# Second attention's last eight turns: rows of the output projection in portions of six products, the next row split during the portions, begun sooner

## The chip, the cores and the metric

The kernel runs on one core of one Trainium2 chip. The metric is the device time of one execution in microseconds (us); three runs were timed. A profiled execution gives a trace of every engine: PE (TensorE, with its weight loads as PEld), DVE (VectorE), ACT (ScalarE), POOL (GpSimd), and SP, which here only issues DMAs.

## The reference

Four layers with residuals on one sequence of 2048 tokens and 640 channels: attention, state space convolution, attention, convolution. The attention is the layer that matters here:

```
def _A_ref(x, wqkv, wo):
    B, S, D = x.shape
    H = 32
    Dh = D // H
    qkv = (lambda x, *d: x.transpose(*d))((x @ wqkv).reshape(B, S, 3, H, Dh), 2, 0, 3, 1, 4)
    q, k, v = qkv[0], qkv[1], qkv[2]
    scores = jnp.einsum("bhqd,bhkd->bhqk", q, k) * (Dh ** -0.5)
    p = _softmax(scores, axis=-1)
    o = jnp.einsum("bhqk,bhkd->bhqd", p, v)
    return (lambda x, *d: x.transpose(*d))(o, 0, 2, 1, 3).reshape(B, S, D) @ wo
...
x = x + _A_ref(_layernorm(x, axis=-1), A_wqkv, A_wo)
x = x + _B_ref(_layernorm(x, axis=-1), B_log_A_real, B_A_imag, B_C_real, B_C_imag, B_log_dt, B_D_skip)
x = x + _A_ref(_layernorm(x, axis=-1), A_wqkv, A_wo)
x = x + _B_ref(_layernorm(x, axis=-1), B_log_A_real, B_A_imag, B_C_real, B_C_imag, B_log_dt, B_D_skip)
```

32 heads of 20 channels; `_B_ref` is a long convolution, done by transforms. The last product, `o @ wo`, is the output projection that the change moves about.

## The kernel before

**Turns.** The attention works on groups of four heads (`g`, 0 to 7) and quarters of the queries (`qb`, 0 to 3, 512 queries each). A group and a quarter are a *turn*; there are 32, and the last eight of the second attention go through the quarters with groups 6 and 7 alternating, so that whole quarters of the sequence become final one after the other. A turn has 16 steps over the keys, of 128 keys each. A step makes two score tiles `S` (two heads each, 128 keys by 1024, eight small matmuls), ACT takes the exponential of each into a tile `pt`, and a value group `pa<-pt,V` sums the four heads' outputs. `S` has two buffers in PSUM, so a third score waits until the first exponential has read its tile. `pt` has seven buffers. A turn therefore has 32 scores, 32 exponentials and 16 value groups.

**Order.** PE's instructions are chained in the order in which they are written, and the writer goes by a plan: the class `Plan` keeps estimated times `plan.pe`, `plan.act`, `plan.dve`, which are advanced by fixed costs (0.22 for a score, 0.92 for an exponential, 0.865 for a value group). After each score, `fill` writes a value group that is due and then, with `slot(plan.act - 0.5)`, pieces of other work as long as the planned PE time, with the piece's cost, stays 0.5 under the planned ACT time. What such a piece is comes from a generator in `todo`: first the projections of the attention itself (`jobs`), and in the last turns of the second attention the rows of the output projection (`rows_out`). Work of DVE, POOL and SP that has a due time is kept in the list `later`, which `drain_later` empties.

**Rows of the output projection.** A *row* `s` (0 to 15) is 128 tokens. The attention's scaled outputs are stored to DRAM as `ot` (channels by tokens). `Rows.load` fetches a row's channels into a tile `otl`, in two parts: channel blocks 0 to 2 and 3 to 4 (of five blocks of 128), since the second part needs groups 6 and 7. `Rows.split` cuts it into two float parts `oh` and `ol` (a copy and a subtraction on DVE). With the weights cut likewise into `woh` and `wol` a block takes three products, `ol` by `woh`, `oh` by `woh`, `oh` by `wol`, for each half of 320 output columns: 18 products for a part of three blocks, 12 for one of two, 30 for a whole row. They add up in a PSUM tile `m`, and DVE adds each half to the residual `x`. When both parts of a row are done, `stats_of` and `normalise` make its layer norm on DVE for the convolution that follows (`uhx`, `ulx`).

`rows_out` begins 30 planned microseconds after it is set up, yields a portion of four products to `slot` at a time, and prices it so:

```
part_ = mm[k:k + 4]
cost = 0.25 + 0.147 * len(part_)
yield t0, cost, k > 0, tuple(hf for hf in range(2) if k <= half * hf < k + 4)
```

Before it comes `end_jobs`, where `prefetch` loads the weights `wo`; their five splits are put into `later` at 8, 12, 16, 20 and 24 planned microseconds.

**Behind the turns.** The last block of the attention (group 7, last quarter) is scaled by `at_once`: a matmul with `dsel` spreads the sums, DVE takes a reciprocal, scales `oc`, and POOL issues the stores to `ot`. Then `out_proj` makes what is left of the projection, in order of rows, into PSUM tiles `po`: a row's `ol` products first, then its `oh` products, the splits now by ACT (`oh`) and DVE (`ol`), two row parts loaded ahead, and each finished row is normalised with the help of ACT (`u`, `uhx`). The last four rows, 12 to 15, need the last block. `psx` is the first stage of the convolution, which takes the normalised rows two by two.

Of the kernel before, what the change touches and what calls it, by code (L numbers as in the profile page):

```python
# [29 lines left out]
NA, NB = 32, 64  # L30
LV = [1.0, 2.0, 4.0, 8.0, 16.0, 32.0, 64.0, 128.0, 256.0, 512.0, 1024.0, 1536.0]
PB = 7
AHEAD = ((0, 0.0), (110, 6.0), (236, 32.0), (364, 59.0), (600, 95.0), (724, 134.0))
BLOCKS = ((0, 128), (128, 32), (160, 128), (288, 128), (416, 128), (544, 96))
NBLK = len(BLOCKS)
# [52 lines left out]
def mha_s4d_kernel(ctx, tc, x_in, wqkv, wo, lar, aim, cr, ci, ldt, dsk,  # L88
# [23 lines left out]
    def pst(pool, *a, **k):  # L112
        return ps_[pool].tile(*a, **k)
# [318 lines left out]
    def attention(x, stats):  # L432
# [522 lines left out]
        def end_jobs():  # L955
# [18 lines left out]
                xpools.pop().__exit__(None, None, None)  # L974
            rest = []
            made = prefetch(x, rest)
            later.extend((plan.pe + (6.0 + 1.5 * n if first_layer else 8.0 + 4.0 * n), f) for n, f in enumerate(rest))
            later.sort(key=lambda e: e[0])
            return made

        def fill(j):

            if ready:
                t = max(ready[0][0] + 0.15, 0.0 if ready[0][3] else sums_[0])
                if t <= plan.pe + 0.1 or j and len(ready) > 2:
                    plan.on_pe(0.0, t)
                    values(*ready.pop(0)[1:])
            while slot(plan.act - 0.5):
                pass
            drain_later()  # L990
            weave()
# [59 lines left out]
        def rows_out(rows, x, woh, wol):  # L1051

            def ask():
# [1 line left out]
                if item:  # L1055
                    rows.load(item)
                return plan.pe + 6.0
            t, done, parts_done = plan.pe + 30.0, [], set()
            while rows.left or rows.loaded:
                yield t, 0.0, False, ()  # L1060
                if stop:
                    return
                if not rows.loaded:
                    t = ask() - (0.0 if rows.loaded else 4.0)
                    continue
                (s, c0, c1), oh, ol = rows.split(ve.tensor_copy)
                t0, t = plan.dve + 0.2, ask()
                mm = [(hf, a, m, ct) for hf in range(2) for ct in range(c0, c1) for a, m in ((ol, woh), (oh, woh), (oh, wol))]
                half, k, pos = len(mm) // 2, 0, [None, None]
                while k < len(mm):  # L1070
                    part_ = mm[k:k + 4]
                    cost = 0.25 + 0.147 * len(part_)
                    yield t0, cost, k > 0, tuple(hf for hf in range(2) if k <= half * hf < k + 4)
                    plan.on_pe(cost)
                    for hf, a, m, ct in part_:
                        if k % half == 0:
# [6 lines left out]
                    while done:  # L1083
                        hf = done.pop()
                        xs = x[:, s, 320 * hf:320 * hf + 320]
                        evac = lambda: ve.tensor_add(xs, xs, pos[hf])
                        emptied(*((None, evac) if hf else (evac,)))
                if s in parts_done:
                    stats_of(x, s, rows.mv[:, s, :])
                    rows.whole.add(s)  # L1090
                    normalise(rows, x, s)
                parts_done.add(s)

        last[0] = None
        tail, rows, stop = None, None, []
        every = {NBLK - 1, ("v", 3)}
        NG = H // 4
        turns = [(g, qb) for g in range(NG) for qb in range(4)]
# [2 lines left out]
        for n, (g, qb) in enumerate(turns):  # L1101
# [4 lines left out]
            if tail is not None and rows is None and (n == len(turns) - 1 or not first_layer):  # L1106
# [6 lines left out]
                    first = []  # L1113
                else:
                    todo[0], head[0] = rows_out(rows, tail[0], tail[2], tail[3]), None
            pa = [pst("A", [P, 512], F32, tag=f"pa{r}", name=f"pa{r}") for r in range(2)]
            g2, qb2 = turns[n + 1] if n + 1 < len(turns) else (g, 0)
            for kt in range(NI):
# [22 lines left out]
            values(*r_[1:])  # L1141
        if not first_layer:
            stop.append(True)
            first = []
            while head[0] is not None and head[0][1]:
                slot()
            for s in range(NI):
                two = [(s, 0, 3), (s, 3, NCT)]
                if set(two) <= set(rows.left):
# [644 lines left out]
```

## Time and profile before

| | us |
|---|---|
| runs | 2646.05, 2641.08, 2644.88 |
| median | 2644.88 |
| profiled execution: span from its first to its last instruction | 2647.0 |
| second attention's turns, from the first exponential's start | 1469.26 |
| its last eight turns, from the first exponential's start | 2203.02 |

The page of the profile states the span of the profiled execution and no other time of it.

```profile
PE 2492.4 (94%) x52388; PEld 1409.8 (53%) x52388; DVE 1519.5 (57%) x3430; ACT 2344.0 (89%) x2763; POOL 801.7 (30%) x1230
...
PE   6899999999999999899898999999999998999898
...
ACT  7899999999999999655665899999999999999574
```

The first line has each engine's busy time, share of the span and instructions. In the strips each digit is the busy share of one fortieth of the span (66 us), in tenths. The last eight turns are slices 34 to 37 of 40, counted from 1, and the projection behind them is slice 38. In rows of the trace, `x8` counts instructions, a time in us comes first, and brackets hold the idle time of the engine before the row and what ended it. The kernel computes in fp32 with two passes for some products, so that the profile counts 16 instructions of a value group where the program has 8.

### The profile page before, as it was taken

To read this page: it belongs to the slowest core of one execution; us is meant where nothing else is said; L and a number is where in the kernel's file an instruction comes from. 1 tells how busy PE (TensorE), PEld (TensorE's weight loads), DVE (VectorE), ACT (ScalarE), POOL (GpSimd) and SP (SyncE) were. 2 spreads that over 40 slices of the span, in tenths; PEclk is the share of its full clock that TensorE was granted. 3 is DMA by queue.
4 is the path that set the end of the run, shared out by engine and by line. 5 is a ranking of instruction groups with operands and counts; after the bars stand their busy time and mean duration, and the time that the engine had idled before them with its cause. 6 is when DMAs were issued, how large, how long until landed. Compare 5 with 4: busy or idle time off the path is not lost.

```text
span 2647.0 us, 118800 instructions
## 1 busy us (share of the span) xinstructions
PE 2492.4 (94%) x52388; PEld 1409.8 (53%) x52388; DVE 1519.5 (57%) x3430; ACT 2344.0 (89%) x2763; POOL 801.7 (30%) x1230
## 2 busy tenths in 40 slices
PE   6899999999999999899898999999999998999898
PEld 3444444454444444587896544454444443444898
DVE  7587777777765887577786323232232222143875
ACT  7899999999999999655665899999999999999574
POOL 1123333233323332111681122222222223222285
PEclk9999999999999999999999999999999999999999
DMA  6522222322222221654652111121121113222466
GB/s 206 189 53 77 68 74 62 82 65 63 61 54 59 53 63 38 234 206 163 213 173 64 47 53 50 51 60 45 45 66 39 50 34 87 71 66 61 137 190 184
DMA packets 188158, 241.99 MB, mean 91 GB/s; under 512 B 43504, under 2 KB 128816, under 8 KB 186224
## 3 DMA queue, kind: packets, MB, share of 16 engines
q1 hardware_dynamic: 151936, 188.28, 22.6%
q0 software_dynamic: 35696, 46.01, 7.4%
q8 instruction: 413, 6.77, 1.1%
q14 instruction: 113, 0.93, 0.1%
HBM read 158.16 MB, written 76.00 MB: 88 GB/s over the span
## 4 chain that ended last, share of the span: by engine, by line
ACT 59%; PE 20%; issue 10%; DVE 3%; DMA 2%; POOL 1%; SPq 0%; ACTq 0%; POOLq 0%; DVEq 0%
ACT pt L78 57%; PE psy L1430 3%; PE pa L903 2%; PE psv L1430 2%; PE po L193 2%; PE psx L1430 2%; PE S L868 2%; PE pst L1452 1%; PE pkx L193 1%; PE pv L586 1%; PE m L620 1%; PE pkt L196 1%; PE pq L773 1%; DMA kb<-khb 1%; DMA kop<-ks 1%
## 5 line engine op out<-in xcount | busy, mean ns | idle before, releaser
L78 ACT ACTIVATE pt<-S 128x1024 f32<-128x1024 f32 x2048 | 1927.7, 1033 | 27.9 <-PE S L868 15.5
L903 PE MATMUL pa<-pt,V 64*32 64x512 f32 x16384 | 1096.9, 589 | 1.4 <-DVE oc L78 1.4
L868 PE MATMUL S<-qop,kop 61*32 61x512 f16 x16384 | 877.2, 380 | 82.7 <-ACT pt L78 67.8
L868 PEld LDWEIGHTS <-kop 61*32 61x32 f16 x16384 | 366.9, 89 | 737.3 <-issue 619.2
L903 PEld LDWEIGHTS pa<-pt,V 64*32 64x32 f32 x16384 | 312.7, 106 | 72.0 <-issue 8.6
L78 POOL DMA_DIRECT2D dn<-oc x248 | 122.7, 501 | 574.2 <-DVE oc L78 574.1
L78 DVE TENSOR_SCALAR qc<-m 128x512 f32<-128x512 f32 (+1 forms) x68 | 46.8, 688 | 312.0 <-PE m L620 312.0
L78 POOL DMA_DIRECT2D db<-dn x248 | 125.4, 512 | 141.5 <-DMA dn<-dr 136.9
L78 POOL DMA_DIRECT2D ot<-oc x256 | 130.5, 517 | 88.4 <-DVE oc L78 55.5
L620 PE MATMUL m<-xl,wh 64*32 64x512 f16 x2560 | 143.8, 376 | 0.3 <-issue 0.3
L620 PE MATMUL m<-xh,wh 64*32 64x512 f16 x2560 | 144.1, 378 | 0.0
L620 PE MATMUL m<-xh,wl 64*32 64x512 f16 x2560 | 143.8, 377 | 0.0
L78 DVE COPY oc<-pa 128x512 f32<-128x512 f32 x64 | 44.2, 690 | 172.9 <-PE pa L903 168.9
L78 ACT COPY xt<-pst 128x1024 f16<-128x1024 f16 x80 | 81.3, 1016 | 60.8 <-PE pst L1452 60.8
L620 PEld LDWEIGHTS <-wh 64*32 64x32 f16 x5120 | 90.3, 93 | 73.3 <-issue 30.8
L78 POOL DMA_DIRECT2D dn<-dr x62 | 34.6, 558 | 287.3 <-DVE dr L78 248.6
L1480 POOL TENSOR_TENSOR kb<-t,kb 128x512 f32<-128x512 f32 x76 | 97.2, 1280 | 65.2 <-DVE t L78 40.8
L78 DVE TENSOR_SCALAR V<-m 128x160 f32<-128x160 f32 x64 | 20.7, 324 | 163.4 <-PE m L586 163.4
L78 DVE TENSOR_TENSOR kb<-ktab 128x512 f32<-128x512 f32 x160 | 106.2, 683 | 0.0
L586 PEld LDWEIGHTS <-xh 128*128 128x128 f16 x960 | 79.7, 98 | 46.7 <-issue 31.4
L1480 POOL TENSOR_TENSOR ka<-ka,kb 128x512 f32<-128x512 f32 x76 | 97.5, 1283 | 6.0
L337 PEld LDWEIGHTS m<-kb,ka 128*32 128x32 f32 x3840 | 60.8, 109 | 71.0 <-issue 52.4
(312 smaller groups left out, 3936.4 us busy)
## 6 DMA issues: line engine op xcount, KB each, us to landing
ka<-kha SPq DMA_DIRECT2D x80, 256.0 KB
kb<-khb SPq DMA_DIRECT2D x80, 256.0 KB
db<-dn POOLq DMA_DIRECT2D x248, 64.0 KB, 3.2
kop<-ks SPq DMA_DIRECT2D x176, 80.0 KB
kpw<-wd POOLq DMA_DIRECT2D x60, 192.0 KB, 3.9
qop<-qs SPq DMA_DIRECT2D x256, 40.0 KB
ot<-oc POOLq DMA_DIRECT2D x256, 40.0 KB, 3.0
kha<-kn SPq DMA_DIRECT2D x20, 512.0 KB
```

The lines of the kernel that those rows point to most:

```text
L78: made = f(out, *a, **k)
L193: chain(te.matmul(*a, **k))
L196: chain(te.transpose(*a, **k))
L337: chain(te.matmul(ps[32 * j:32 * j + 32, c8, :], a[n][:, ch, :], b[n][:, dd, :], start=(n == 0), stop=(n == 2), tile_position=(0, 32 * j)))
L586: chain(te.matmul(ps[:, :n], a_[:, ct, sl], m[:, ct, :], start=(k == 0), stop=(k == 14)))
L620: chain(te.matmul(ps[r][32 * t:32 * t + 32, :], a_[rows, ct, 32 * u:32 * u + 32], m[rows, ct, 512 * v:512 * v + 512], start=(k == 0), stop ...
L773: te.matmul(pq, a_[:, ct, :], m[:, ct, sl], start=(n == 0), stop=(n == 14))
L868: chain(te.matmul(S[32 * t:32 * t + 32, 512 * r:512 * r + 512], kt_[rows, kc + 32 * t:kc + 32 * t + 32], qt[rows, :], start=True, stop=Tru ...
L903: chain(te.matmul(pa[r][32 * j:32 * j + 32, :], V[rows, kt, VP * h:VP * h + 32], pts[j // 2][rows, 512 * (j % 2):512 * (j % 2) + 512], sta ...
L1430: at("pe", te.matmul(*a, **k))
L1452: at("pe", te.transpose(pt[:, k, g, :], of_group(x1[k], 4 * q + g), id16))
L1480: at("pool", getattr(ge, f)(*a))
```

## The change

Portions of the projection in the turns are six products instead of four (`RUN`), with a smaller price in the plan (1.03 for six, where four had 0.838). The weights' splits come due earlier (5 to 15 planned microseconds instead of 8 to 24), and the rows begin 18 instead of 30 planned microseconds after the set-up. The next part is split while the portions of the present one go on (`split_next`; `parted` holds a part that is split and not yet multiplied), and the limit in `fill` becomes 0.25 instead of 0.5 in these turns (`margin`). A part that is split when the turns end is handed to `out_proj` as its first.

```diff
+RUN = 6
...
-            later.extend((plan.pe + (6.0 + 1.5 * n if first_layer else 8.0 + 4.0 * n), f) for n, f in enumerate(rest))
+            later.extend((plan.pe + (6.0 + 1.5 * n if first_layer else 5.0 + 2.5 * n), f) for n, f in enumerate(rest))
...
-            while slot(plan.act - 0.5):
+            while slot(plan.act - margin[0]):
...
-            t, done, parts_done = plan.pe + 30.0, [], set()
-            while rows.left or rows.loaded:
-                yield t, 0.0, False, ()
+
+            def split_next():
+                made = rows.split(ve.tensor_copy)
+                parted.append((plan.dve + 0.2, made))
+                return ask()
+            t, done, parts_done = plan.pe + 18.0, [], set()
+            while rows.left or rows.loaded or parted:
+                yield (0.0 if parted else t), 0.0, False, ()
                 if stop:
                     return
-                if not rows.loaded:
-                    t = ask() - (0.0 if rows.loaded else 4.0)
-                    continue
-                (s, c0, c1), oh, ol = rows.split(ve.tensor_copy)
-                t0, t = plan.dve + 0.2, ask()
+                if not parted:
+                    if not rows.loaded:
+                        t = ask() - (0.0 if rows.loaded else 4.0)
+                        continue
+                    t = split_next()
+                t0, ((s, c0, c1), oh, ol) = parted.pop()
...
-                    part_ = mm[k:k + 4]
-                    cost = 0.25 + 0.147 * len(part_)
-                    yield t0, cost, k > 0, tuple(hf for hf in range(2) if k <= half * hf < k + 4)
+                    part_ = mm[k:k + RUN]
+                    cost = 0.16 + 0.145 * len(part_)
+                    yield t0, cost, k > 0, tuple(hf for hf in range(2) if k <= half * hf < k + RUN)
...
+                    if not rows.loaded and not parted:
+                        t = ask()
+                    elif rows.loaded and not parted and t <= plan.pe:
+                        t = split_next()
...
+        parted, margin = [], [0.5]
...
+                    margin[0] = 0.25
...
             stop.append(True)
-            first = []
             while head[0] is not None and head[0][1]:
                 slot()
+            first = [e[1] for e in parted]
```

The order of the built program is the same up to the second attention's last turns. On PE, a portion and the scores around it, before (numbers behind names are buffers; `LDWEIGHTS kop` and `MATMUL S` are one small part of a score):

```order
L868 MATMUL S<-qop_31439,kop_31436 32x512
L1078 MATMUL m_52761<-woh,ol 128x320
L1078 MATMUL m_52761<-woh,oh 128x320
L1078 MATMUL m_52761<-wol,oh 128x320
L1078 MATMUL m_52761<-woh,ol 128x320
L868 LDWEIGHTS kop_31438
```

And at the same kind of place afterwards:

```order
L869 MATMUL S<-qop_31439,kop_31435 32x512
L1085 MATMUL m_52776<-woh,ol 128x320
L1085 MATMUL m_52776<-woh,oh 128x320
L1085 MATMUL m_52776<-wol,oh 128x320
L1085 MATMUL m_52776<-woh,ol 128x320
L1085 MATMUL m_52776<-woh,oh 128x320
L1085 MATMUL m_52776<-wol,oh 128x320
L869 LDWEIGHTS kop_31437
```

Six products stand between two scores where four stood. With S for a score, P for a value group and a number for the products of a portion, most of a turn reads S 4 S P S S P before and S 6 S P S S P afterwards. Counted over the order, the eight turns have 56 portions with 212 products before and 57 with 342 afterwards; behind the last score follow 10 and 6, and `out_proj` has 258 and 132.

On DVE, behind the last value group: the last block's outputs `oc`, what stands ahead of the reciprocal, and the scaling with `db`. Before:

```order
L78 TENSOR_TENSOR oc<-oc,pa_54267 128x512
L78 TENSOR_TENSOR x<-x,m_54749 128x320
L78 TENSOR_TENSOR x<-x,m_54866 128x320
L78 BN_STATS st_54878<-x 128x6 x2
L78 TENSOR_TENSOR ol<-otl,oh 128x384
L78 BN_AGGR mvx<-st_54878 128x2
L78 TENSOR_TENSOR oc<-oc,db 128x512
L78 TENSOR_TENSOR x<-x,po 128x320
L78 TENSOR_SCALAR db<-m_54886 128x512
L78 TENSOR_TENSOR ol<-otl,oh 128x384
L78 RECIPROCAL db<-db 128x512
```

Afterwards:

```order
L79 TENSOR_TENSOR oc<-oc,pa_54519 128x512
L79 TENSOR_TENSOR x<-x,m_55091 128x320
L79 TENSOR_TENSOR oc<-oc,db 128x512
L79 TENSOR_TENSOR ol<-otl,oh 128x256
L79 TENSOR_SCALAR db<-m_55135 128x512
L79 TENSOR_TENSOR x<-x,po 128x320
L79 RECIPROCAL db<-db 128x512
```

One add, two statistics, a mean and one split less stand ahead of the reciprocal.

On SP's queue, behind the last score's operands: the loads of the rows that are left (`otl`, 3, 2 or 5 blocks of 128 channels) among the convolution's constants `e1s`, `f2s`, `id`, `fa`. Before:

```order
L78 DMA otl<-ot 128x3x128 x2
L78 DMA e1s<-in_c_e 128x2x1024
L78 DMA otl<-ot 128x5x128
L78 DMA e1s<-in_c_e 128x2x1024
L78 DMA otl<-ot 128x5x128
L78 DMA e1s<-in_c_e 128x2x1024 x2
L78 DMA otl<-ot 128x5x128
L78 DMA f2s<-in_c_f 128x64
L78 DMA id_54937<-in_c_id 128x128
L78 DMA fa<-in_c_fa 128x128
L78 DMA otl<-ot 128x5x128 x4
```

Afterwards:

```order
L79 DMA otl<-ot 128x2x128 x3
L79 DMA e1s<-in_c_e 128x2x1024
L79 DMA otl<-ot 128x2x128
L79 DMA e1s<-in_c_e 128x2x1024 x3
L79 DMA f2s<-in_c_f 128x64
L79 DMA id_55166<-in_c_id 128x128
L79 DMA fa<-in_c_fa 128x128
L79 DMA otl<-ot 128x2x128 x2
L79 DMA otl<-ot 128x5x128 x2
```

Seven whole rows (9 to 15) are loaded there before, the last four of them (12 to 15) in one run; afterwards only rows 14 and 15 are whole, and rows 8 to 13 are halves of two blocks. In both, rows 12 to 15 stand last.

## The prediction

> **What bounds the kernel now.** I read the page first: its header, its chain and its groups.
>
> ```profile
> span 2647.0 us, 118800 instructions
> ...
> ACT 59%; PE 20%; issue 10%; DVE 3%; DMA 2%; POOL 1%; SPq 0%; ACTq 0%; POOLq 0%; DVEq 0%
> ...
> L78 ACT ACTIVATE pt<-S 128x1024 f32<-128x1024 f32 x2048 | 1927.7, 1033 | 27.9 <-PE S L868 15.5
> ...
> L868 PE MATMUL S<-qop,kop 61*32 61x512 f16 x16384 | 877.2, 380 | 82.7 <-ACT pt L78 67.8
> ```
>
> The exponentials on ScalarE are the path, and both attentions run at their rate. That is an average, so next I read the stage that is edited: stretches around the second attention's last turns and the projection behind them.
>
> ```profile
> 2205.00:2235.00 30.00, 24.44 (x520) 10.10 (x520) 9.39 (x21) 29.80 (x33) 7.56 (x14) 1.00 0.35 97
> ...
> 2357.00:2387.00 30.00, 28.93 (x541) 12.88 (x540) 19.68 (x72) 29.47 (x32) 7.12 (x14) 1.00 0.25 71
> ...
> 2449.00:2470.00 21.00, 20.70 (x167) 18.10 (x152) 18.79 (x56) 6.90 (x12) 4.01 (x8) 1.00 0.57 178
> 2470.00:2500.00 30.00, 25.09 (x187) 24.75 (x186) 26.96 (x77) 16.72 (x26) 11.66 (x8) 0.96 0.28 86
> ```
>
> Columns are PE, weight loads, DVE, ACT, POOL. In the turns ACT is full; PE goes from 24.4 of 30 us without portions to 28.9 with them, so little room is left there. Behind the attention (from 2449) PE and DVE are both full. The question is therefore what a product costs inside the turns and what it is worth outside. The exponentials, merged in the timeline, give the first half: one turn without portions, then the seven with them.
>
> ```profile
> 2203.02 29.73 ACT L78 ACTIVATE pt<-S 128x1024 f32<-128x1024 f32 x32
> ...
> 2232.62 217.23 ACT L78 ACTIVATE pt<-S 128x1024 f32<-128x1024 f32 x224
> ```
>
> Taking off the 0.1 us by which the last exponential outlasts its place in the row, a bare turn is 29.63 us (0.926 an exponential, 3.70 for four) and seven turns are 217.1. Portions cost 217.1 - 7 x 29.63 = **9.7 us** already. The built order has 56 portions there, so 0.17 us each: ACT is not untouched by them.
>
> **The change part by part.**
>
> *Portions of six.* One cycle of the present pattern, PE's timeline:
>
> ```profile
> 2284.24 0.41 PE L868 MATMUL S<-qop,kop 61*32 61x512 f16 x8
> 2284.59 0.42 PE L1078 MATMUL m<-woh,oh 128*128 128x320 f32 x1
> 2284.84 0.31 PE L1078 MATMUL m<-wol,oh 128*128 128x320 f32 x1
> 2284.99 0.31 PE L1078 MATMUL m<-woh,ol 128*128 128x320 f32 x1
> 2285.13 0.31 PE L1078 MATMUL m<-woh,oh 128*128 128x320 f32 x1
> 2285.37 0.41 PE L868 MATMUL S<-qop,kop 61*32 61x512 f16 x8
> 2285.60 1.04 PE L903 MATMUL pa<-pt,V 64*32 64x512 f32 x16
> 2286.46 0.94 PE L868 MATMUL S<-qop,kop 61*32 61x512 f16 x16
> 2287.21 1.05 PE L903 MATMUL pa<-pt,V 64*32 64x512 f32 x16
> 2288.07 0.41 PE L868 MATMUL S<-qop,kop 61*32 61x512 f16 x8
> 2288.41 0.41 PE L1078 MATMUL m<-wol,oh 128*128 128x320 f32 x1
> ...
> 2285.91 1.03 ACT L78 ACTIVATE pt<-S 128x1024 f32<-128x1024 f32 x1
> ```
>
> Four scores, two value groups and one portion repeat after 2288.41 - 2284.59 = 3.82 us, against 3.70 for four exponentials in a bare turn. This is a loop, not PE's sum of work. Only two S tiles exist. The score begun at 2285.37 is read by the exponential at 2285.91, which frees its tile at 2286.94; the row of sixteen score products at 2286.46 is two groups, of which the second has to wait for that, at about 2286.99. From there follow the value group (2287.21), the score at 2288.07 and, 1.13 us behind that score (2285.37 - 2284.24), the score after the next portion. So the loop is 1.62 (score, exponential, free tile) + 1.08 (score and value group) + 1.13 (score and portion) = 3.83. Each product within a portion adds its start-to-start time, 2285.13 - 2284.99 = 0.147 (two steps 0.15 and 0.14; ten products at the end go at the same pace). A portion of two would leave 3.53 and hide; four stick out by 0.12 to 0.2; **the fifth and sixth add 0.29 whole**, because the slack is used up. The cycle becomes 4.11.
>
> The built order places portions of six where the portions of four stood, mostly one to four scores: eight or nine a turn. It has 57 of them (342 products) before the last score, against 56 (212 products, six of the portions only pairs). At 4.11 instead of 3.82 per cycle, eight cycles a turn: 8 x 0.29 = 2.3 us a turn, 16.3 over seven turns. The short portions that become six add some tenths, the one portion in the turn before 0.4; the turn starts, where two portions stand close together, are alike in both orders. I take **+16.5**, with 14.5 (only the 50 full portions grow: 50 x 0.29) and 18.5 (pairs growing to six cost the whole 0.41 over a bare cycle) as ends.
>
> *Splits during portions, weights earlier, margin 0.25.* The two rows of a split, in these turns:
>
> ```profile
> L78 DVE TENSOR_TENSOR ol<-otl,oh 128x256 fp32r<-128x256 f32 x8 | 3.4, 425 | 0.3
> ...
> L78 DVE CAST oh<-otl 128x256 fp32r<-128x256 f32 x8 | 2.1, 258 | 0.0
> ```
>
> That is 0.7 us a part on DVE, which is busy under two thirds of these stretches; moved between the two halves of a row they hide behind the portions. Without that cover each would hold PE for about 0.7 us. The five weight splits go earlier by up to 14 us, on a DVE busy 9.4 of 30 us: nothing. Their loads and the first row loads pass the kop and qop loads on SP's queue by a few places; no score of these turns waits for a DMA now, so nothing, at most one late load of about 2 us. The smaller margin is what lets the longer portions be placed; its cost is in the loop above.
>
> *What is left behind the attention.* There 258 products remain, 132 afterwards:
>
> ```profile
> L1338 PE MATMUL po<-wol,oh 128*128 128x320 f32 x86 | 25.4, 309 | 0.0
> ...
> 2475.77 1.63 PE L1338 MATMUL po<-woh,ol 128*128 128x320 f32 x10
> ...
> 2493.33 0.31 PE L1338 MATMUL po<-wol,oh 128*128 128x320 f32 x1
> ...
> 2497.71 0.47 DVE L78 TENSOR_TENSOR x<-x,po 128x320 f32<-128x320 f32 x1
> ```
>
> (86 of each of three kinds.) 126 fewer at 0.147 are 18.5 us of PE. But the last four rows need the last block of the attention, which comes by another way:
>
> ```profile
> 2456.88 3.35 DVE L78 RECIPROCAL db<-db 128x512 f32<-128x512 f32 x1
> 2460.48 0.68 DVE L78 TENSOR_TENSOR oc<-oc,db 128x512 f32<-128x512 f32 x1
> ...
> 2461.45 4.01 POOL L78 DMA_DIRECT2D ot<-oc  x8 [25.15 <-DVE nr L78]
> ...
> 2468.93 10.03 SPq L78 DMA_DIRECT2D otl<-ot  x4
> ...
> 2473.31 0.81 DVE L78 TENSOR_TENSOR ol<-otl,oh 128x640 fp32r<-128x640 f32 x1
> ```
>
> Reciprocal, scaling, eight stores, the load of row 12, its split: ready at 2474.1, and PE, coming from row 11, takes it up at 2475.77. Today this chain is hidden with 1.7 us to spare. Afterwards PE has only rows 8 to 11 in halves (48 products, 7 us) before it, so **the chain ends last**. On the clock of before: the reciprocal loses about 1 us of DVE work ahead of it, so the load goes at about 2468 and the split could end at 2473. DVE's own order agrees with that. The prices of a row's steps:
>
> ```profile
> L78 DVE TENSOR_TENSOR x<-x,po 128x320 f32<-128x320 f32 x18 | 8.5, 475 | 0.1
> L78 DVE BATCH_NORM_STATS2 st<-x 128x6 f32<-128x320 f32 x18 | 8.5, 481 | 0.1
> ```
>
> Between scaling and that split stand, by the built order, eight adds and eight statistics (0.47 each by busy time over count, 7.5), some fourteen small steps (0.15 to 0.17, 2.2) and the splits, means and convolution parts of four rows (about 3.5): 13 us from 2459.8, to 2473. I take 2473.9 for PE's start on row 12, since ACT now does two rows' u ahead of that split. Rows 12 and 13 are 24 products, 3.5 us; the splits of rows 14 and 15 stand behind row 13's adds, 1.5 us; then 60 products, 8.8 us: 2487.7. PE would end 5.8 us sooner than its 2493.5, not 18.5. Before, the last add (2497.71) came 4.2 us behind PE because DVE was full; with less for DVE to do it can follow within 0.5, at 2488.2: 9.5 us sooner.
>
> From this goes what idling costs PE. The first-stage products of the convolution in this same tail:
>
> ```profile
> 2493.48 0.23 PE L1430 MATMUL psx<-uhx,e1s 128*128 128x128 f16 x1
> ...
> 2494.78 0.22 PE L1430 MATMUL psx<-uhx,e1s 128*128 128x128 f16 x1
> 2499.91 0.27 PE L1430 MATMUL psx<-uhx,e1s 128*128 128x128 f16 x1 [4.91 <-DVE x L78]
> ...
> 2502.21 0.31 PE L1430 MATMUL psx<-ulx,e1s 128*128 128x128 f16 x1
> ```
>
> Twenty-four of them in 1.30 us ahead of an idle time of 4.9, then 22 in 2.30: 0.056 against 0.105 each. After the change rows 8 to 11 would be through by about 2464 (the last of them is split behind the scaling, at 2461), and PE would idle some 9 us ahead of row 12; so its 24 products could take twice 3.5 us. Bounds 0 and 3.5; I take 1.5, since part of it falls into the wait for rows 14 and 15. The tail's gain is then **8**, with ends 4 (the store chain not sooner, cold products in full) and 11.
>
> The Trainium skill, TensorE: Matmul & The Clock Gate, section What's actually happening, states that the array falls to half its clock after an idle window of about 3.4 us and comes back after about 3.4 us of work. The doubled step behind the idle 4.9 us agrees with it. By that page's window the loss here would be an estimated 1.7 us, and the sum 0.2 us higher.
>
> Sum: +16.5 - 8 = **+8.5 us**. The page gives only the span, 2647.0, which lies 2.1 us above the median of the three times (2644.88); I add the difference to the median: **2653.4**.
>
> **The rivals.**
>
> *The added products hide* (it ends on the other side). If PE could run ahead over more than the two S tiles, a portion of six would only lengthen PE's own work: 32 scores x 0.21, 16 value groups x 0.86 and 8 portions x 1.2 us make 30.1 us a turn, below today's 31.0, and the attention would stay as it is. Then the tail's 8 us is pure gain: 2636.9. It decides at a cycle of 3.7 us: if the cycle stays at 3.82, this holds. For it: PE's busy share is under 97%. Against it: the cycle of 3.82 is already over the 3.70 of four exponentials, and closes to 0.01 us with no term that could shrink.
>
> *The tail is PE's alone.* If the last block's chain kept ahead of PE, all 18.5 us would come off: +16.5 - 18.5 = -2, 2642.9. For it: PE is full there today. Against: row 12's split, ready 1.7 us before it is needed, cannot move by 12.
>
> *The tail gains nothing*, because the chain to the last rows, DVE's normalising and a cold PE together end as late as now: 2661.4. For it: DVE is busy 27 of 30 us there; against: eight row parts are left to split and add instead of ten, and eight rows to normalise instead of nine.
>
> That the change does not do as it says is excluded by the built order: the portions are six, the splits lie between.
>
> **How the numbers follow.** Forecast case (attention +14.5 to +18.5, tail -4 to -11, so 2648 to 2659): 0.74. Hidden: 0.09. PE's tail: 0.09. No gain in the tail: 0.08. The range takes the forecast's and the second rival's, 2643 to 2660, which leaves out some 0.17. A measurement of this kernel tells 0.2% (5.3 us) from no change, so the lines are 2639.6 and 2650.2. About 0.11 of the forecast case lies under +5.3. Slower: 0.63 + 0.08 = 0.71; within: 0.11 + 0.09 = 0.20; faster 0.09.
>
> **What would show it.** Right: portions repeating at 4.1 us, turns of 33 us instead of 31, the last exponential about 16 us later; behind it PE idle for several us ahead of row 12's products with the wait put to DVE, ACT or a load, and the way from the start of the last exponential (2232.62 + 217.23 - 1.03 = 2448.82) to the last `x<-x,po` some 8 us shorter than its 48.9. Wrong: a cycle of 3.8 with six products would mean that a tile is freed earlier than I read; PE without idle time up to the last row would mean that the chain of the last block is shorter; a score waiting for a `kop` or `qop` load would mean that the passed loads cost.

## The result, and the profile after

The changed kernel takes 2670.61 us (median of 5 runs, 2666.01 to 2673.89), beside 2645.62 us before on the same chip (5 runs, 2641.08 to 2647.68): a ratio of 1.0099, with a 95% interval of 1.0086 to 1.0112 (the two medians alone give 1.0094). It is slower, as forecast, but by 25 us and not by 8.5, and above the range. The profiled execution took 2673.89 us.

Its page, at the lines shown of before (the last is a group of instructions: count, busy time and mean, then the idle time ahead of them and what ended most of it):

```profile
span 2672.0 us, 118840 instructions
...
ACT 54%; PE 25%; issue 9%; DVE 3%; DMA 3%; POOL 1%; SPq 0%; ACTq 0%; POOLq 0%; DVEq 0%
...
L79 ACT ACTIVATE pt<-S 128x1024 f32<-128x1024 f32 x2048 | 1932.7, 1033 | 54.8 <-PE S L869 42.6
```

The exponentials have lost ground: ACT stands idle for 54.8 us ahead of them instead of 27.9, and 42.6 of it ends with a score. PE's share of the chain grows from 20 to 25%, and DMA's from 2 to 3%.

Next, the edited stage in four stretches: the first of the last eight turns (turn 24 of 0 to 31), the three behind it, the two after these, and the last two up to the start of the last exponential. Each row has the length, then the busy times of PE, weight loads, DVE, ACT and POOL, the granted clock, the DMA share and GB/s. Before:

```profile
2203.02:2232.62 29.60, 24.15 (x512) 9.97 (x512) 9.25 (x20) 29.57 (x34) 7.56 (x14) 1.00 0.34 97
2232.62:2325.57 92.95, 87.86 (x1621) 39.02 (x1621) 15.58 (x34) 91.46 (x97) 21.64 (x42) 1.00 0.26 69
2325.57:2387.40 61.83, 59.41 (x1087) 26.57 (x1087) 33.16 (x118) 60.80 (x66) 14.25 (x28) 1.00 0.24 68
2387.40:2448.82 61.42, 58.89 (x1074) 26.72 (x1081) 23.08 (x73) 60.28 (x64) 14.33 (x28) 1.00 0.21 59
```

And after:

```profile
2205.49:2243.98 38.49, 27.65 (x526) 11.64 (x533) 9.99 (x22) 29.99 (x33) 7.78 (x14) 0.92 0.31 92
2243.98:2343.27 99.29, 96.01 (x1675) 45.76 (x1660) 21.06 (x47) 93.13 (x97) 21.59 (x42) 0.99 0.24 65
2343.27:2414.86 71.59, 66.84 (x1121) 31.91 (x1121) 38.60 (x134) 62.37 (x66) 14.55 (x28) 0.98 0.23 64
2414.86:2480.96 66.10, 64.18 (x1110) 31.83 (x1117) 33.63 (x117) 61.52 (x64) 14.22 (x28) 1.00 0.22 60
```

The sums are 245.8 and 275.5 us, so the attention is **29.7 us longer** (forecast 16.5). From the last exponential's start to the end of the span it is 191.1, against 198.2 (2672.0 - 2480.96 and 2647.0 - 2448.82, with the spans taken to a hundredth): the tail is **7.1 us shorter** (forecast 8). Turn 24 has 38.49 us, of which ACT works 29.99; before, it was a bare turn. Turns 28 and 29 have 71.59, some 5 more than the two behind them. What ACT waits for in turn 24 is in its timeline (brackets: idle time before, and what ended it):

```profile
2223.31 7.60 ACT L79 ACTIVATE pt<-S 128x1024 f32<-128x1024 f32 x8 [1.87 <-PE S L869]
...
2241.87 1.02 ACT L79 ACTIVATE pt<-S 128x1024 f32<-128x1024 f32 x1 [5.46 <-PE S L869]
2243.98 2.95 ACT L79 ACTIVATE pt<-S 128x1024 f32<-128x1024 f32 x3 [1.08 <-PE S L869]
```

Each is a wait for a score, so PE's timeline says what the scores waited for (the last two rows belong to the tail):

```profile
2222.78 0.41 PE L869 MATMUL S<-qop,kop 61*32 61x512 f16 x7 [1.43 <-DMA kop<-ks]
...
2239.22 0.60 PE L1085 MATMUL m<-woh,ol 128*128 128x320 f32 x1 [4.02 <-DVE ol L79]
2239.62 0.47 PE L1085 MATMUL m<-woh,oh 128*128 128x320 f32 x1
2239.89 0.47 PE L1085 MATMUL m<-wol,oh 128*128 128x320 f32 x1
...
2293.18 0.42 PE L1085 MATMUL m<-woh,ol 128*128 128x320 f32 x1
...
2297.29 0.42 PE L1085 MATMUL m<-woh,ol 128*128 128x320 f32 x1
...
2503.68 1.44 PE L1351 MATMUL po<-woh,ol 128*128 128x320 f32 x4 [2.46 <-DVE ol L79]
...
2510.63 1.73 PE L1351 MATMUL po<-woh,ol 128*128 128x320 f32 x10 [1.31 <-DVE ol L79]
```

At 2222.78 a score waits for a `kop` load. At 2239.22 the first portion waits for its row's split: it stands in PE's order ahead of the next score, so ACT waits with it. The rows at 2293.18 and 2297.29 start two portions, one cycle apart. Turns 28 and 29 have the same two kinds of wait; the last row is ACT's wait behind the second of them, its longest there:

```profile
2375.55 0.42 PE L1085 MATMUL m<-woh,ol 128*128 128x320 f32 x1 [1.04 <-DVE ol L79]
...
2397.70 0.41 PE L869 MATMUL S<-qop,kop 61*32 61x512 f16 x7 [1.46 <-DMA kop<-ks]
...
2398.22 1.02 ACT L79 ACTIVATE pt<-S 128x1024 f32<-128x1024 f32 x1 [2.49 <-PE S L869]
```

Both kinds lead to DMA issues, and these to SP's timeline:

```profile
2201.86 9.05 SPq L79 DMA_DIRECT2D otl<-in_wo  x3
2211.00 4.83 SPq L79 DMA_DIRECT2D kop<-ks  x8
...
2234.39 5.11 SPq L79 DMA_DIRECT2D otl<-ot  x3
...
2371.09 16.27 SPq L79 DMA_DIRECT2D otl<-ot  x3
2387.47 4.71 SPq L79 DMA_DIRECT2D kop<-ks  x8
```

The same place before:

```profile
2199.30 0.83 SPq L78 DMA_DIRECT2D otl<-in_wo  x2
2201.07 4.71 SPq L78 DMA_DIRECT2D kop<-ks  x8
2209.06 7.41 SPq L78 DMA_DIRECT2D otl<-in_wo  x3
```

A row merges several issues, and it is long when one of them waits. Three weight loads take 9.05 us, and behind them stand the eight `kop` loads for the second half of this turn's keys; before, only the two weight loads that find free buffers went ahead of these. In turns 28 and 29 three row loads take 16.27 us, with turn 29's eight `kop` loads behind them. Before, such a group of eight went out 1.9 us ahead of its turn's first exponential (2201.07 against 2203.02 in turn 24, 2354.56 against 2356.49 in turn 29); now it goes out 5.5 us (2211.00 - 2205.49) and 9.2 us (2387.47 - 2378.25) behind it. The view of the waits on SP's queue, in the stretches 2195 to 2245 and 2365 to 2400, names what was waited for (sum, times, longest):

```profile
SPq L79 <- DVE wx L79: 6.2, 1, 6.2
```

```profile
SPq L79 <- DMA ot<-oc: 14.8, 3, 10.5
```

The third weight load waits for one of the two `otl` buffers. The view names the DVE instruction of that moment; the buffer comes free when the first weight split is through, in DVE's timeline at 2209.72 + 0.83 = 2210.55:

```profile
2209.72 0.83 DVE L79 TENSOR_TENSOR wol<-otl,woh 128x640 fp32r<-128x640 f32 x1
```

And a row load waits for a block's stores to `ot`.

### The profile page after: what moved, and what is told of

Same layout as the page of the kernel before. It is cut to its first block, busy times and chain, and to the rows that moved or that the text cites. A ratio compares the mean times of both kernels' runs of the same rounds, so it can differ in the third digit from the quotient of the medians.

```text
span 2672.0 us, 118840 instructions
## 1 busy us (share of the span) xinstructions
PE 2500.8 (94%) x52388; PEld 1410.4 (53%) x52388; DVE 1529.4 (57%) x3465; ACT 2344.2 (88%) x2757; POOL 800.5 (30%) x1229
## 4 chain that ended last, share of the span: by engine, by line
ACT 54%; PE 25%; issue 9%; DVE 3%; DMA 3%; POOL 1%; SPq 0%; ACTq 0%; POOLq 0%; DVEq 0%
ACT pt L79 52%; PE pa L904 4%; PE S L869 3%; PE psy L1443 2%; PE psv L1443 2%; PE m L1085 2%; PE po L194 2%; PE psx L1443 2%; DMA kop<-ks 1%; PE pst L1465 1%; PE pkx L194 1%; PE pv L587 1%; PE pkt L197 1%; PE pq L774 1%; PE m L621 1%
## 5 line engine op out<-in xcount | busy, mean ns | idle before, releaser
L79 ACT ACTIVATE pt<-S 128x1024 f32<-128x1024 f32 x2048 | 1932.7, 1033 | 54.8 <-PE S L869 42.6
L79 POOL DMA_DIRECT2D dn<-dr x62 | 34.6, 558 | 304.4 <-DVE dr L79 259.8
```

Of the source, the lines that this page charges most:

```text
L79: made = f(out, *a, **k)
```

## The experiments

Twelve kernels ran, each beside the kernel before (2645.8 to 2646.1 us). Two theories on the 13 us of attention above the forecast: the **queue theory** (loads in another order on SP, and a portion that stands in PE's order ahead of its row's data) and the **cycle theory** (the longer portions and the splits between them cost more than the loop says). Totals below are medians; lengths of stretches are from each kernel's one profiled execution, whose total can lie some 6 us off its median (2660.12 against 2653.91 in one case), while its undisturbed turns repeat within 0.1 us. Turn 24 starts anywhere between 2194.88 and 2205.49 us, although hardly anything ahead of it differs: a total carries this, a stretch does not.

| run | median | ratio, 95% | attention | tail |
|---|---|---|---|---|
| changed kernel | 2670.61 | 1.0086 to 1.0112 | 275.5 | 191.1 |
| late_both | 2662.10 | 1.0057 to 1.0083 | 266.8 | 191.9 |
| late_weights | 2665.13 | 1.0064 to 1.0090 | 272.3 | 191.9 |
| late_begin | 2662.57 | 1.0053 to 1.0077 | 267.3 | 190.7 |
| six_in_place | 2665.20 | 1.0063 to 1.0089 | 261.0 | 201.0 |
| rows_on_pool | 2653.91 | 1.0016 to 1.0040 | 261.1 | 191.6 |
| early_on_pool | 2656.96 | 1.0027 to 1.0055 | 264.5 | 191.3 |
| begin18_alone | 2653.26 | 1.0015 to 1.0033 | 251.3 | 199.2 |
| weights_alone | 2648.39 | 1.0001 to 1.0019 | 247.8 | 201.2 |
| four_late | 2653.34 | 1.0021 to 1.0046 | 247.0 | 205.9 |
| four_late_pool | 2650.99 | 1.0011 to 1.0032 | 245.4 | 204.7 |
| three_late | 2651.33 | 1.0011 to 1.0029 | 241.9 | 208.0 |
| none_in_turns | 2670.71 | 1.0074 to 1.0105 | 237.0 | 232.8 |
| before | 2645.62 | | 245.8 | 198.2 |

**The two times undone, together and apart** (on the changed kernel; late_both has both edits, late_weights the first, late_begin the second):

```diff
-... else 5.0 + 2.5 * n), f) for n, f in enumerate(rest))
+... else 8.0 + 4.0 * n), f) for n, f in enumerate(rest))
...
-            t, done, parts_done = plan.pe + 18.0, [], set()
+            t, done, parts_done = plan.pe + 30.0, [], set()
```

> The changed kernel with its two due times put back: rows begin at +30.0, weight splits at 8.0 + 4.0n. Portions stay six (55 of them, none in turn 24), margin 0.25 and the split between the halves stay. Queue theory: the 13 us above the forecast of the attention come from loads that stand in another order on SP, 8.4 of them in turn 24 (1.9 us kop, 5.5 and 1.1 us first row part). With SP's order before turn 25 as it was (2 weight loads, 8 kop loads, 3 weight loads, 1 row load), turn 24 is a bare turn of 29.6 us again and the time falls from 2670.6 to 2660 to 2663. Cycle theory (rival): the excess lies in the portions of six themselves and in the splits between them; then the time stays at 2669 to 2671.

> The changed kernel with only the weight splits back at 8.0 + 4.0n; rows still begin at +18.0. PE's order is that of the change (57 portions, one in turn 24). Queue theory: the 8 kop loads are issued ahead of the third weight load again, so no score of turn 24 waits for kop (-1.9 us); SP reaches the first row load some 3 us sooner, so the wait of the first portion shrinks from 5.5 to about 2 to 3 us: 2664 to 2667. Cycle theory: 2669 to 2671.

> The changed kernel with only the rows' begin back at +30.0; weight splits early. Queue theory: no portion in turn 24, so the 5.5 + 1.1 us in which PE waits for the first row part go; the scores' wait for kop (1.9 us) stays, since the third weight load still stands ahead of the 8 kop loads: 2663 to 2665. Cycle theory: 2669 to 2671. If late_weights and late_begin each bring nearly the whole gain of late_both, the two waits are one (SP late by the first makes the second).

All three fell as the queue theory said, late_begin 0.4 us below its range. Turn 24 (first stretch) in late_both, then in late_weights, then in late_begin:

```profile
2201.47:2231.07 29.60, 24.15 (x512) 9.99 (x512) 9.16 (x20) 29.57 (x33) 7.76 (x14) 1.00 0.34 100
```

```profile
2199.44:2234.54 35.10, 26.34 (x526) 11.03 (x533) 10.09 (x22) 29.81 (x34) 7.55 (x14) 0.97 0.33 97
```

```profile
2199.00:2230.12 31.12, 24.42 (x512) 9.79 (x511) 9.15 (x20) 29.75 (x33) 7.43 (x14) 1.00 0.34 96
```

A bare 29.60 with both undone; 1.5 us more from the early weights alone, 5.5 from the early begin alone, 8.9 from both. Together they cost 1.9 us more than the two alone. SP, late by the first, issues the first row load later (2234.39 in the change, 2227.04 in late_weights, whose turn had begun 6.0 us earlier, so 1.3 later within the turn). In late_weights the first portion still waits 3.78 us, where 2 to 3 were expected: most of that wait needs the early begin alone.

**Portions of six alone**, on the kernel before, with the planned cost of four so that the places stay:

```diff
-                    part_ = mm[k:k + 4]
-                    cost = 0.25 + 0.147 * len(part_)
-                    yield t0, cost, k > 0, tuple(hf for hf in range(2) if k <= half * hf < k + 4)
+                    part_ = mm[k:k + 6]
+                    cost = 0.838
+                    yield t0, cost, k > 0, tuple(hf for hf in range(2) if k <= half * hf < k + 6)
```

> The kernel before with one edit: portions of six in the places where portions of four stood (their planned cost left at 0.838 us), all times, splits and margin as before; 55 portions of six before the last exponential. Loop term of the forecast: each adds 0.29 us, so the attention +15 to +16, and the tail is 7 us shorter: 2645.6 + 15.5 - 7 = 2654 (2651 to 2657). Cycle theory: a portion of six costs 0.5 us more than one of four, and the kernel stands at 2663 to 2668. If longer portions hid: 2639.

The total fell where the cycle theory put it (2665.2), and yet that theory is wrong: the attention is 261.0, 15.2 us above before, as the loop said. The tail missed: 201.0 with 114 products fewer, where 7 us less were expected. So the attention has to be read apart from the tail; no total tells the theories from each other.

**Row loads on another queue** (on late_both; the loads in the turns only):

```diff
-                sy.dma_start(o[:, c0:c1], ot[...
+                (sy if first_layer or stop else ge).dma_start(o[:, c0:c1], ot[...
```

> late_both with one more edit: the row loads of the last eight turns go out on POOL's queue instead of SP's. In late_both's trace the third of three row loads waits 10.4 us on SP for the stores of a block, 8 kop loads stand behind it, and turns 28 and 29 are 34.9 and 37.5 us instead of 33.2. Queue theory: with the rows off SP no score waits for kop, turns 28 and 29 become 33.3 us, attention 266.8 - 5.6 = 261.2, and the time falls from 2662.1 to 2656 to 2658. Rival: the long turns come from the split on DVE or from the portions that stand there; then 2662 stays, with PE waiting for DVE's ol or for pt there. A second risk: POOL, waiting for the stores, issues the denominators' loads later and the splits come late; then the stall only changes its place.

Turns 28 and 29, in late_both and here:

```profile
2329.70:2402.12 72.42, 66.75 (x1121) 31.92 (x1121) 38.58 (x134) 62.24 (x65) 14.49 (x28) 0.98 0.23 63
```

```profile
2333.67:2400.36 66.69, 64.35 (x1121) 31.05 (x1121) 38.70 (x134) 62.10 (x65) 19.43 (x36) 1.00 0.24 69
```

Same work on PE (1121 instructions), 5.7 us less; the attention is 261.1, expected 261.2. With no `kop` load behind a waiting row load the stall is gone, and it did not come back elsewhere. The total is lower than expected (2653.9, expected 2656 to 2658). This stall is not one of the two early times, which late_both has undone. It is absent in six_in_place too (66.48), which has portions of six but neither the splits during portions nor the smaller margin. With these a third row load goes out ahead of the `kop` loads (three in 17.01 us, at 2357.55 in late_both; in six_in_place two in 0.91, at 2357.57, and the third behind the `kop` loads). Which of the two brings it forward no run separates.

**The change's early times, with weight and row loads on POOL's queue** (the edit above and the same for the weight load):

```diff
-            sy.dma_start(wt, wo[ct * P:ct * P + P, :])
+            ge.dma_start(wt, wo[ct * P:ct * P + P, :])
```

> The changed kernel with all its early times; the five weight loads and the row loads of the last turns go out on POOL's queue instead of SP's. PE's order is that of the change (57 portions of six, one in turn 24). Queue theory: of the 14.5 us of stalls the kop waits go (1.9 in turn 24, some 5 in turns 28 and 29); the first portion of turn 24 still stands in PE's order ahead of a score, and how long it waits depends on when its row's load lands: if the load goes out as soon as it is due, 0 to 3 us instead of 6.5. Attention 262 to 266, time 2656 to 2660. If the 6.5 us of the first portion have nothing to do with SP's queue, turn 24 stays near 35 us and the time near 2662. Rival: POOL held up by the weight loads' wait for a buffer makes the denominators late, and the time stays at 2665 or above.

PE's portions are those of the change, one in turn 24 included:

```profile
2194.88:2226.10 31.22, 25.30 (x518) 10.66 (x518) 10.11 (x22) 29.92 (x34) 11.38 (x20) 1.00 0.38 107
...
2326.58:2393.26 66.68, 64.35 (x1121) 31.05 (x1121) 38.64 (x134) 62.10 (x65) 19.46 (x36) 1.00 0.25 69
```

Turn 24 falls from 38.49 to 31.22 and turns 28 and 29 from 71.59 to 66.68; the attention is 264.5, 11.0 us below the change's, and the median 13.7 below; the tails agree (191.1 and 191.3), so the 2.7 us between the two figures are not of the edited stage. The three turns between take 100.48 us instead of 99.29, and scores wait there 1.2 us for `qop` loads: not all of the stall is gone. This is the cleanest test: the same times and the same order of portions, and only the queue differs.

**Each early time alone, on the kernel before** (18.0 for 30.0; 5.0 + 2.5n for 8.0 + 4.0n):

> The kernel before with one edit: rows begin at +18.0 instead of +30.0. Portions of four, 60 before the last exponential instead of 57, the first of them in turn 24. SP gets two row loads ahead of the 8 kop loads of turn 24 instead of one. Queue theory: the first portion waits in PE's order for its row as in the change, so turn 24 is 3 to 6 us longer than 29.6, with nothing but the time of begin changed: 2648 to 2652. If the wait in turn 24 needs the other parts of the change: 2644 to 2647.

> The kernel before with one edit: the weight splits at 5.0 + 2.5n instead of 8.0 + 4.0n. SP's order becomes 3 weight loads, 8 kop loads, 2 weight loads, as in the change; PE's order is unchanged. Queue theory: the third weight load waits for a buffer until the second split is through on DVE, the 8 kop loads wait behind it, and turn 24 is 1.3 to 1.9 us longer (late_begin: 31.12 instead of 29.60): 2647 to 2648. The forecast costed this at nothing: 2645.8.

Turn 24 is 35.9 us in the first, with one wait of 5.35 us in it, and 31.15 in the second, with one of 1.31 (in ACT's timelines; that of the first):

```profile
2234.56 1.02 ACT L78 ACTIVATE pt<-S 128x1024 f32<-128x1024 f32 x1 [5.35 <-PE S L868]
```

So both stalls come with portions of four too. The wait for the row's first part was a little above what was expected (6.3 us in the turn, total 2653.3 against 2648 to 2652), and so was weights_alone's total (2648.4 against 2647 to 2648). Of weights_alone's 2.3 us (2646.06 beside it), the 1.5 in turn 24 are the queue; its tail is 3 us longer than before's with the same order of work there, so a single tail is known to about 3 us.

**The price of a product in a portion**: portions of four and of three in the places of the six (late_both with `RUN = 4` or `RUN = 3` and `cost = 1.03`), four_late with row loads on POOL, and none at all (portions of six with the cost of before's formula, 1.13, which its margin never lets in).

> late_both with portions of four in the places of the portions of six (planned cost kept at 1.03 us): 54 portions, 204 products, 276 left behind the attention instead of 150. It is the kernel before with the split between the halves, the smaller margin and the carried part. six_in_place had 114 products fewer behind the attention than the kernel before and yet its last row addition came 1.7 us later after the last exponential, so fewer products alone bring nothing there. Order theory: the tail's 7 us come from DVE's work in another order (the reciprocal of the last block starts 1.6 us sooner) and stay with portions of four: attention 245 plus 0 to 3 for late loads, tail 191 to 193, so 2639 to 2643. Product theory: the tail's gain belongs to the longer portions, and is gone: 2646 to 2651.

> four_late with the row loads on POOL's queue. Queue theory: what four_late has of late kop loads (0 to 3 us in turns 28 to 30) goes, and nothing else changes: equal to four_late or up to 3 us below it. If POOL's waits for stores delay the rows, portions wait for ol and it is slower than four_late.

> late_both with portions of three in the same places (54 portions, 162 products). Loop term: the cycle is 1.62 + 1.08 + (1.13 - 0.147) = 3.68 us, just under the 3.70 of four exponentials, so the portions hide: turns of 29.7 to 30 us, attention 237 to 239, against about 245 with portions of four. Behind the attention 318 products are left, 42 more than with four (6.2 us if PE is the bound there, 0 if DVE and the last block's chain are): 2634 to 2645. If the cost of a portion were in proportion to its products, without slack (rival), the attention would be 242 to 243.

> The kernel before with portions of six whose planned cost (1.13 us) no longer fits its margin of 0.5: no portion is placed before the last exponential, and all 462 products but the 18 behind it are left for the tail. It measures both prices of a product. In the turns: 8 bare turns of 29.65, attention 237 instead of 245.8 (the forecast's 9.7 us for 57 portions). Behind: 204 products more; at 0.147 each the tail is 30 us longer than 198.2, so 2645.8 - 9 + 30 = 2667. If DVE and the last block's chain were the bound of the tail and PE not (as the 114 products that six_in_place left out suggest), it would be shorter: 2650 to 2660.

Turns 26 and 27 together, sixteen places, with none, three, four and six products (none_in_turns, three_late, four_late, six_in_place):

```profile
2260.88:2320.08 59.20, 48.30 (x1024) 19.95 (x1024) 4.82 (x10) 59.14 (x65) 14.20 (x28) 1.00 0.22 61
```

```profile
2258.87:2319.25 60.38, 57.20 (x1073) 25.49 (x1073) 10.65 (x23) 60.20 (x65) 16.46 (x32) 1.00 0.24 65
```

```profile
2257.78:2319.52 61.74, 59.06 (x1083) 26.45 (x1083) 9.94 (x22) 60.75 (x66) 15.07 (x30) 1.00 0.24 68
```

```profile
2263.14:2329.62 66.48, 64.42 (x1121) 30.87 (x1121) 14.59 (x33) 62.32 (x66) 14.24 (x28) 1.00 0.24 68
```

Over the bare turns a portion of three costs 1.18 / 16 = 0.07 us, one of four 0.16, one of six 0.455. These are means, and four_late's is low: its sixteen portions hold 58 products, for three of them are pairs. The cycle of four scores, two value groups and one portion has no pairs in it; its median in the turns with portions is 3.77 us with three products (three_late), 3.82 with four (four_late) and 4.11 with six (six_in_place). The fourth product thus costs 0.05 us and the fifth and sixth 0.14 each: the slack is used up at about four, and from there a product costs its whole time. Three do not quite hide (30.2 a turn, expected 29.7 to 30; a cycle of 3.77 where the loop gives 3.68), and the attention of 241.9 touches the rival's range, partly through two lone waits of 0.77 us in the last turns; but in proportion to four, a portion of three would cost 0.12.

The tails were mostly missed, and with them the totals of four_late (2653.3; 2639 to 2643 or 2646 to 2651 was expected) and three_late (2651.3; 2634 to 2645). four_late kept the split between the halves and the carried part, and its tail is 205.9 and not 191 to 193; three_late's is 208.0 with 42 products more. In four_late the last row addition comes 49.2 us behind the last exponential's start, about where before's does (48.9); the other 7 us lie behind the projection, where PE's granted clock is 0.60 and 0.55 in the twenty microseconds from 2494.70. four_late_pool took 1.6 us off four_late's attention, as expected (turn 29 was 33.4 there and is 31.3 here). none_in_turns leaves 204 products more than before behind the attention and its tail is 34.6 us longer, 0.17 each, a little above the 30 us expected. None of the twelve beats the kernel before.

## Why the forecast was right in sign and too small

- **The path and the portions: right.** The cycle is 2297.29 - 2293.18 = 4.11 us, as worked out. Portions of six without late loads lengthen the attention by 15.2 us (six_in_place) and 15.3 (rows_on_pool) with 55 of them; with the 57 that were counted, at 0.455, it would be 16.1. The forecast had 16.5, with ends 14.5 and 18.5.
- **The step that failed** is this: "Their loads and the first row loads pass the kop and qop loads on SP's queue by a few places; no score of these turns waits for a DMA now, so nothing, at most one late load of about 2 us." The waits cost 8.9 us in turn 24, 5.1 in turns 28 and 29 and 0.6 in the three turns between, by the stretches of the change against six_in_place, 14.5 together (the last two turns give 0.2 back, and some 0.9 are the two portions more). On another queue the same loads at the same times give 2656.96 for 2670.61, and take 11.0 of the 14.5 us away. Three things lay under the step. The count of places did not matter, but what the passing load itself waits for: the third weight load a buffer (6.2 us), a row load a block's stores (10.5). The trace of before had shown it: its `otl<-in_wo` row of three loads is 7.41 us long, and harmless there because the `kop` loads are ahead of it. And the first portion, begun 12 us sooner, stands in PE's order ahead of a score, so its row's load, issued behind twenty `kop` and `qop` loads, holds up ACT. The 5.1 us of turns 28 and 29 belong to a sentence next to it: splits moved between the halves of a row "hide behind the portions". That priced DVE, and not the row load that goes out sooner with such a split.
- That no score waits for a DMA is true of these turns before, and says nothing of afterwards: the eight `kop` loads had their slack from the place that they were moved out of. The forecast named the sign to look for (a score waiting for a `kop` load) and bounded it at one late load of about 2 us. The `kop` wait of turn 24 is that large (1.87 us of ACT); the portion's wait and those of turns 28 and 29 are what the bound left out.
- **The tail: right in size, half right in cause.** The last block's chain does end last: PE waits 2.46 and 1.31 us for `ol` ahead of rows 12 and 14, its clock is at 0.60 and 0.72 between 2500 and 2510. From row 11's last product to row 12's first pass 7.75 us (2495.93 to 2503.68; some 9 were forecast), and the next sixteen products take 4.31 us (to 2507.99) where 16 x 0.147 is 2.35: 2.0 us lost, 1.5 forecast. In all, from the last exponential's start to the last row addition it is 2521.41 - 2480.96 = 40.5 us instead of 48.9. DVE's timeline has the chain's first link and its last:

```profile
2487.41 3.35 DVE L79 RECIPROCAL db<-db 128x512 f32<-128x512 f32 x1
...
2521.41 0.48 DVE L79 TENSOR_TENSOR x<-x,po 128x320 f32<-128x320 f32 x1
```

The reciprocal starts 6.45 us behind the last exponential's start; before it was 8.06 (2456.88 - 2448.82), and in six_in_place 9.97, behind a row's normalising, with the split of row 12 late in turn:

```profile
2472.35 3.34 DVE L78 RECIPROCAL db<-db 128x512 f32<-128x512 f32 x1
...
2489.37 2.62 DVE L78 TENSOR_TENSOR ol<-otl,oh 128x640 fp32r<-128x640 f32 x2
```

  Fewer products alone brought nothing (six_in_place, with PE's clock at 0.50 from 2482.38 to 2492.38), and the split order alone neither (four_late); the five kernels of the experiments with both have tails of 190.7 to 191.9. That DVE's order ahead of the reciprocal decides it is read from the traces; no run changed that order alone, and it stays open. An early reciprocal is not enough: in three_late it starts 5.62 us behind the last exponential's start, and with 318 products left the last row addition comes at 57.0.
- **The rivals.** That the products hide is refuted by the cycle of 4.11, that the tail is PE's alone by six_in_place, that it gains nothing by 191.1 against 198.2 (and 40.5 against 48.9 to the last row addition, since a whole tail is known to about 3 us). The missing rival was a queue.
- **The sum.** 15.2 + 14.5 - 7.1 = 22.6 by the traces, to which 2.5 us come that the profiled execution of the change had lost before turn 24 (2205.49 against 2203.02), where the order is the same. Without the queue's term the forecast stands: rows_on_pool 2653.9 for 2653.4, and early_on_pool 2657.0. That the first comes within 0.5 us is partly luck: it has 55 portions and not 57, and its six executions spread from 2652.4 to 2660.1.

## What to carry to other kernels

An edit that moves a DMA issue on an in-order queue is priced by what that issue itself will wait for (a buffer, a store that it reads) and by who stands behind it, not by the number of places; before calling it free, look for long rows of that queue in the trace of before. Work that is slipped between the links of a loop is nearly free until the loop's slack is used up, and costs its whole time from there (here at four products, 0.14 us each), hardly less than afterwards (0.17 in none_in_turns): past that point there is little to win by moving it. And a portion that is placed ahead of the critical engine's next input needs its data early by the worst case of the queue, not by the plan's.

## What the hardware showed beyond that

The longest wait of PE cost more than its length. Behind the 4.02 us wait in turn 24 the products follow each other at 2239.89 - 2239.62 = 0.27 us instead of 0.147, and the granted clock stays near half from 2238 to about 2245, most of it behind the first product (columns as above):

```profile
2238.00:2240.00 2.00, 0.78 (x3) 0.81 (x4) 0.92 (x2) 0.00 (x0) 0.00 (x0) 0.54 0.01 2
2240.00:2242.00 2.00, 2.00 (x21) 1.15 (x27) 0.00 (x0) 0.13 (x1) 0.00 (x0) 0.50 0.44 127
2242.00:2244.00 2.00, 2.00 (x32) 0.53 (x24) 0.00 (x0) 0.92 (x2) 0.00 (x0) 0.50 0.22 66
2244.00:2246.00 2.00, 2.00 (x34) 0.75 (x19) 0.38 (x1) 2.00 (x3) 0.00 (x0) 0.76 0.27 82
```

The 1.08 us that ACT waits again behind the 5.46 fall into that time. In late_weights the wait was 3.78 us, the portion behind it ran at full pace, and the clock fell to 0.53 only afterwards (2232 to 2234). The Trainium skill, TensorE: Matmul & The Clock Gate, section What's actually happening, has half clock after an idle window of about 3.4 us, and both waits agree with that. A third does not: in turn 29 PE's longest wait is the 1.46 us at 2397.70, with only one product in the 2 us ahead of it, and the granted clock is 0.79 from 2398 to 2399 and 0.50 from there to 2402. In turn 24 the like (0.74 and 1.43 us, with one product between, up to 2222.78) left it at 1.00. So less than 3.4 us of idle time is no assurance here, and what decides between these two the runs do not show.

The other surprise is what a second queue is worth: 11.0 us of attention (13.7 by the medians) for loads that carry the same bytes at the same planned times. The Trainium skill, Trainium Kernel Development and Optimization, section Key Constraints, says that issuing DMAs from several engines "only saves the sequencer's issue time". The runs differ from that where an issue waits: on SP alone, while one row load waited 10.5 us for stores, eight `kop` loads that had gone out 1.9 us ahead of their turn before came 9.2 us into it.
